# Splitting weights on VectorE instead of GpSimd in the later stages of an attention, feed-forward and expert kernel, with three weight blocks split early

## The chip, the cores and the metric

The kernel runs on one core of one Trainium2 chip. The metric is device time in microseconds (us) of one execution, lower is better. The core has TensorE (PE in the rows, with PEld for its weight loads), VectorE (DVE), ScalarE (ACT), GpSimd (POOL) and SyncE (SP, which issues most transfers). Each engine works through its own instructions in the order of the program and waits for the others by semaphores.

## The reference

Three parts follow one another; the output of each is the input of the next.

```python
# 1. attention: batch 4, 8 heads, 1152 keys, head size 64; queries pooled in twos
q_pool = q.reshape(B, H, S // 2, 2, D).mean(axis=3)
scores = scale * q_pool @ k^T;  attn = softmax(scores);  x = attn @ v      # x: 2304 tokens x 512
# 2. feed-forward on all tokens, 512 -> 2048 -> 512, w_in and w_out are float64
h = x @ w_in;  g = h * sigmoid(1.702 * h);  x = g @ w_out
# 3. experts: tokens with x @ w_skip > 0 go to the best of 8 experts, the rest stay as they are
out = x;  out[sel] += gate * (relu(x[sel] @ w1[e]) @ w2[e])                 # 512 -> 1024 -> 512
```

## The kernel before, in words

Products are made from two parts of each operand, a high one (the operand rounded to the 4-byte type that TensorE multiplies) and a low one (the rest), so that `a*b` is taken as `ah*bh + ah*bl + al*bh`. Making the two parts is called a split: ScalarE writes the high part, and VectorE or GpSimd writes the low one. `nc.gpsimd` is GpSimd, `V` is VectorE.

**Attention** (`attention`, L124) goes over 16 pairs of heads. One pair has 14 score units (`UNITS`, `NU`), and a counter `g` runs over all units. At each `g` the loop at L365 issues one score unit (matmuls, then an exponential on ScalarE into tiles `E`), one unit of row maxima for a pair 19 units ahead (matmul, then a VectorE reduction, L230), now and then the product with `v` (L306), and a unit of row sums: GpSimd adds up the tiles `E` (`sum_unit`, L284 and L286) and finishes the denominators `ds` (through the agenda, so that their line is L69). `den` (L316) turns `ds` into the matmul `dn`. Other work hangs on the agenda `ag`, a list of (step, function) run when `g` reaches the step; `quiet` picks steps with little VectorE work.

**Splitting float64 weights** (`wsplit`, L422). The weights come as pairs of 32-bit words. A unit `u` is one of 32 tiles of 128 x 512 weights (w_in or w_out of one of 16 blocks `fb`). It takes seven VectorE operations on words (L450, L451, L452, L440, L454, L455, L444), two ScalarE copies (L441 for the low words, L446 for the high part) and one product for the low part (L445), which GpSimd makes for all blocks but block 0. With `EARLY = 1` the two units of block 0 are split during attention (`weights`, L341); the other thirty are split in the first chunk of the feed-forward stage, whose buffers (`m_raw`, `m_tmp`) are opened after attention is closed.

**Feed-forward** (`ffn`, L484). The 2304 tokens go in six chunks (`CH`: 768, 384, 256, 256, 256, 384). The first has 32 steps (16 blocks, two pieces of 384 tokens); a step is `layer1` (12 matmuls into `h`, then sigmoid on ScalarE, `g = h * g` on VectorE, the high part `gh` on ScalarE, the low part `gl`: GpSimd in the first chunk, VectorE later) and, two steps behind, `layer2` (9 matmuls). There are two `h` buffers, so that the matmuls of a step need the `g` of the step two before. `fill(k)` issues the next k waiting VectorE items between these. In the first chunk one unit of weights is split in each step, and the high part of a unit is put into the next step (`ag.at(ag.now + 1, put)`). The tokens of the next chunk are loaded, normalised (`xnorm`, on GpSimd) and split in the last blocks.

**Experts** (`experts`, L841). Slots follow one another, one expert each, with tiles of up to 128 tokens (`tokens_tile`, L908): 24 matmuls up, relu, transposes, 24 matmuls down, `yo` (L957), and a scatter by GpSimd. In the first tile of a slot the 16 weight tiles of the next expert are split (`splits`, L892; L800 is the high part on ScalarE, L801 the low one); every third low part is GpSimd's, which also issues the gathers (L867) and scatters (L958) of tokens. A VectorE operation writes the second half of the relu (L947).

## Time and profile before

| | us |
|---|---|
| median of 3 runs (lowest to highest) | 1119.11 (1115.97 to 1127.57) |
| the profiled execution's own time | 1114.21 |
| its span, from the first to the last instruction | 1112.4 |
| attention, 0 to 450.5: PE / DVE / POOL busy | 433.71 / 324.39 / 383.67 |
| first chunk of feed-forward, 450.5 to 625.3 | 145.33 / 157.21 / 80.39 |
| other chunks, 625.3 to 903 | 275.66 / 199.75 / 31.26 |
| experts, 903 to 1112.4 | 163.18 / 125.56 / 85.74 |

The rows further down are of four kinds. A row of a timeline is: start, duration (us), engine, line, operation, output and inputs with their shapes, a count, and in brackets how long the engine sat idle before it and what ended that. A row of a stretch is: the stretch, its length, then for PE, PEld, DVE, ACT and POOL the busy time with the number of instructions, the granted TensorE clock (1.00 is full speed), the DMA share and GB/s. A row of waits is: engine and line, what it waited for, total us, times, longest. A row of a line is: engine, operation, count, then minimum, median and maximum duration in ns, first and last start, shape.

### The profile page before, as it was taken

The page shows a single profiled execution, that of the slowest core. Times are in us where ns is not written, and L with a number is a line of the kernel's source. Part 1 is how long each engine was busy: PE and PEld are TensorE (multiplying, and loading weights), DVE is VectorE, ACT ScalarE, POOL GpSimd, SP SyncE. Part 2 cuts the span into 40 slices and gives each one's busy share as a digit, 9 for nine tenths or more (in the row PEclk, how much of TensorE's full clock was granted, in tenths as well). Part 3 has the DMA queues.
Part 4 walks back from the last instruction along what each step waited for, and adds up shares of the span by engine and source line. Part 5 has one row for each costly group of instructions (what it writes and reads, how often), then busy time and mean ns, then how long its engine had stood idle before and what let it go on. Part 6 is the DMA issues. An engine that isn't in the chain of part 4 may idle for free. (4 is left out here: it accounts for less than half of the span.)

```text
span 1112.4 us, 19158 instructions
## 1 busy us (share of the span) xinstructions
PE 1017.9 (91%) x7002; PEld 801.3 (72%) x7002; DVE 806.9 (73%) x1584; ACT 482.1 (43%) x885; POOL 581.1 (52%) x408
## 2 busy tenths in 40 slices
PE   6999999999999999688978999999999989977893
PEld 4766767666776666587867898888889877755672
DVE  6767787778877772699999589787567555578734
ACT  2555555555555545243333332333332334256432
POOL 3698888998999988444445202101110106156413
PEclk9999999999999999889999999999999989988897
DMA  4233332223333210332333420211211326456301
GB/s 154 66 95 80 92 108 77 76 90 91 92 108 93 71 48 27 125 96 95 105 117 100 143 77 20 69 62 31 66 41 55 111 92 215 149 184 214 112 31 39
DMA packets 64325, 103.39 MB, mean 93 GB/s; under 512 B 18630, under 2 KB 34630, under 8 KB 64072
## 3 DMA queue, kind: packets, MB, share of 16 engines
q1 hardware_dynamic: 60148, 96.35, 27.4%
q0 software_dynamic: 3904, 5.15, 1.5%
q8 instruction: 69, 1.13, 0.4%
q14 instruction: 56, 0.46, 0.1%
q10 hardware_dynamic: 148, 0.30, 0.1%
HBM read 90.04 MB, written 17.35 MB: 97 GB/s over the span
## 5 line engine op out<-in xcount | busy, mean ns | idle before, releaser
L230 DVE TENSOR_REDUCE mx<-xs 128x1 f32<-128x384 f32 x432 | 213.0, 549 | 79.5 <-PE xs L227 74.8
L271 ACT ACTIVATE E<-ss 128x640 f32<-128x640 f32 (+1 forms) x224 | 174.0, 786 | 155.3 <-PE ss L270 123.0
L286 POOL TENSOR_TENSOR acc<-acc,E 128x640 f32<-128x640 f32 (+1 forms) x96 | 182.1, 1897 | 19.5 <-ACT E L271 15.4
L563 PE MATMUL h<-xh,wih 128*128 128x384 f32 (+1 forms) x448 | 145.8, 326 | 30.8 <-ACT wih L446 26.0
L306 PE MATMUL av<-E,v 128*64 128x256 f32 (+1 forms) x1152 | 157.1, 413 | 0.0
L563 PE MATMUL h<-xl,wih 128*128 128x384 f32 (+1 forms) x448 | 143.6, 321 | 0.7 <-DVE xl L482 0.6
L563 PE MATMUL h<-xh,wil 128*128 128x384 f32 (+1 forms) x448 | 143.2, 320 | 0.0
L563 PEld LDWEIGHTS h<-xh,wih 128*128 128x128 f32 x448 | 86.7, 194 | 43.0 <-ACT wih L446 31.7
L306 PEld LDWEIGHTS av<-E,v 128*64 128x64 f32 x1152 | 75.7, 136 | 56.0 <-issue 15.1
L587 PE MATMUL acc<-woh,gh 128*128 128x512 f32 x288 | 115.6, 401 | 0.0
L589 PE MATMUL acc<-woh,gl 128*128 128x512 f32 x288 | 115.2, 400 | 0.0
L588 PE MATMUL acc<-wol,gh 128*128 128x512 f32 x288 | 114.9, 399 | 0.0
L227 PE MATMUL xs<-kh,qh 64*128 64x384 f32 x384 | 102.3, 389 | 9.7 <-ACT kh L207 7.2
L270 PE MATMUL ss<-qh,kh 64*128 64x320 f32 (+1 forms) x576 | 107.1, 340 | 0.9 <-ACT E L271 0.9
L270 PE MATMUL ss<-M,ONE 64*128 64x320 f32 (+1 forms) x576 | 95.0, 296 | 2.5 <-DMA M<-ml 2.3
L569 DVE TENSOR_TENSOR g<-h,g 128x384 f32<-128x384 f32 (+1 forms) x112 | 55.8, 498 | 56.0 <-ACT g L568 51.3
L606 DVE CUSTOM_DVE_ANT_0 junk<-xs,wg 128x512 bf16<-128x512 f32 x135 | 94.7, 701 | 2.0
L658 POOL DMA_INDIRECT LIST<-pay,si x18 | 18.3, 1018 | 143.0 <-DVE si L655 75.6
L270 PE MATMUL ss<-qh,kl 64*128 64x320 f32 (+1 forms) x576 | 92.4, 294 | 0.0
L270 PE MATMUL ss<-ql,kh 64*128 64x320 f32 (+1 forms) x576 | 92.4, 294 | 0.0
L568 ACT ACTIVATE g<-h 128x384 f32<-128x384 f32 (+1 forms) x112 | 49.1, 439 | 99.1 <-PE h L563 98.8
L563 PEld LDWEIGHTS h<-xl,wih 128*128 128x128 f32 x448 | 87.0, 194 | 5.2 <-DVE xl L482 1.2
(196 smaller groups left out, 2176.8 us busy)
## 6 DMA issues: line engine op xcount, KB each, us to landing
stage<-w SPq DMA_DIRECT2D x40, 512.0 KB
qd<-qT SPq DMA_DIRECT2D x16, 576.0 KB
v<-v SPq DMA_DIRECT2D x16, 576.0 KB
kr<-kT SPq DMA_DIRECT2D x15, 576.0 KB
wr<-w_in SPq DMA_DIRECT2D x15, 512.0 KB
wr<-w_out SPq DMA_DIRECT2D x15, 512.0 KB
X<-xs SPq DMA_DIRECT2D x18, 256.0 KB
out<-xs SPq DMA_DIRECT2D x18, 256.0 KB
```

Source lines behind the costliest of these rows:

```text
L227: nc.tensor.matmul(ps[:, :384], q, k[:, part * 384:part * 384 + 384], start=True, stop=True)
L230: V.reduce_max(o, ps[:, :384], axis=AX.X)
L270: nc.tensor.matmul(ps[:, u, j * w:j * w + w], k[HALF[u]], q[HALF[u], qs], start=(n == 0), stop=(n == 3))
L271: nc.scalar.activation(place(p, i), ps[:, :, :len(kbs) * w], AF.Exp, scale=0.5 / D ** 0.5)
L286: G.tensor_tensor(d["a"], d["a"], place(p, i), op=ALU.add)
L306: nc.tensor.matmul(d["av"][HALF[u], :w], d["v"][:, u, kb], e[:, u, n * w:n * w + w], start=(kb == 0), stop=(kb == KB - 1))
L563: nc.tensor.matmul(h, a[:, d * P:d * P + P], x, start=(k == 0), stop=(k == 3 * ND - 1))
L569: V.tensor_tensor(g, h, g, op=ALU.mult)
L587: nc.tensor.matmul(acc[t], gh[:, ts], bh, start=(fb == 0), stop=False)
L588: nc.tensor.matmul(acc[t], gh[:, ts], bl, start=False, stop=False)
L589: nc.tensor.matmul(acc[t], gl[:, ts], bh, start=False, stop=(fb == NF - 1))
L606: V.tensor_tensor_reduce(out=junk, in0=R[grp[i]], in1=late["wg"][:, e], op0=ALU.mult, op1=ALU.add, scale=1.0, scalar=0.0, accum_out=R[grp] ...
```

## The change

It has six parts.

1. **Buffers.** The buffers for weight words as loaded (`raw`, three of them) are opened before attention and live until the first chunk ends, so that loads can be issued during attention.
2. **Three early blocks.** `EARLY` is 3. The two units of block 0 are split where they were; units 2 to 5 are loaded and split beside the last pair of heads, from 5 units before it to its end. The loads of units 6 and 7 are issued there too.
3. **A unit's operations.** The first word operation (the absolute value) goes from VectorE to ScalarE (`AF.Abs`), the product for the low part from GpSimd to VectorE. VectorE still has seven operations for a unit. In the first chunk they come from a generator, `blocks`, that takes two units in turn and is not bound to a step: 6 or 7 items in each step.
4. **Feed-forward without GpSimd in the first chunk.** `gl` is always VectorE's, and so is `xnorm` for the second chunk; its load and its split are moved by a step or two.
5. **The end of attention.** For the last pair the sums of units 10 to 13 and the denominators are VectorE's (`G = V`).
6. **Experts.** All 16 low parts of a slot are VectorE's; the second half of the relu is ScalarE's.

```diff
-EARLY = 1
+EARLY = 3
@@ sum_unit
+            G = V if p == N - 1 and i > 8 else nc.gpsimd
@@ attention, agenda
-        for b in range(2 * EARLY):
-            ag.at(NU * 1 + 3 + b * (NU * 3 + 6), weights, b // 2, b % 2)
+        for u in range(2):
+            g = NU * 1 + 3 + u * (NU * 3 + 6)
+            ag.at(g, self.wload, u)
+            ag.at(g + 6, weights, u, lambda j, f: quiet(AV_AT[3:], j, f))
+
+        for u in range(2, 2 * EARLY):
+            g, n = NU * (N - 1) - 5, u - 2
+            ag.at(g - 13 + 4 * n if n < 3 else g + 7, self.wload, u)
+            ag.at(g + 5 * n, weights, u, lambda j, f, g=g + 5 * n: ag.at(g + j * 5 // 7, f))
+        for n in range(2):
+            ag.at(NU * N - 8 + 5 * n, self.wload, 2 * EARLY + n)
@@ wsplit
         def last():
-            V.tensor_scalar(sg, t2, 0xFF800000, None, op0=ALU.bitwise_and)
-            (nc.gpsimd if fb else V).tensor_tensor(lo_t, t1.bitcast(F32), sg.bitcast(F32), op=ALU.mult)
-            put = lambda: nc.scalar.activation(hi_t, t2.bitcast(F32), AF.Copy)
-            put() if ag is None else ag.at(ag.now + 1, put)
+            nc.scalar.activation(hi_t, t2.bitcast(F32), AF.Copy)
+            V.tensor_tensor(lo_t, t1.bitcast(F32), sg.bitcast(F32), op=ALU.mult)
-            lambda: V.tensor_scalar(t2, hi, 0x7FFFFFFF, None, op0=ALU.bitwise_and),
+        nc.scalar.activation(t2.bitcast(F32), hi.bitcast(F32), AF.Abs)
@@ ffn
+        def blocks():
+            end = ()
+            for u in range(2 * EARLY, 2 * NF):
+                if u + 2 < 2 * NF:
+                    self.wload(u + 2)
+                a, b, c, d, e, *new = self.wsplit(u, [tp.tile([P, 512], U32, name=nm, tag=nm) for nm in ("t1", "t2", "sg")])
+                yield from (a, *end[:1], b, c, d, *end[1:], e)
+                end = new
+            yield from end
-            self.xnorm(xa[c, j, pc], xraw.pop((c, j, pc)), c, j, pc, nc.gpsimd)
+            self.xnorm(xa[c, j, pc], xraw.pop((c, j, pc)), c, j, pc, V if c == 1 else nc.gpsimd)
-            (nc.gpsimd if c == 0 else V).tensor_tensor(gl, g, gh, op=ALU.subtract)
+            V.tensor_tensor(gl, g, gh, op=ALU.subtract)
-                    wsplit(2 * (fb + EARLY) + 1 + pc)
-                    fa, fb_ = 3, 4
+                    fa, fb_ = 3, 3 + pc
-                            g0 = first[0, 10] + 2 * j if c == 0 else first[c, 4] + 2 * j
+                            g0 = first[0, 12] + 2 * j - 1 if c == 0 else first[c, 4] + 2 * j
@@ experts
-                lambda q=q: self.expert_split(s, q, stage[q // 2][:, q % 2], nc.gpsimd if q % 3 == 2 else V)
+            return [lambda q=q: self.expert_split(s, q, stage[q // 2][:, q % 2]) for q in range(16)]
-            V.tensor_scalar(h[:, 512:], hp[1], 0.0, None, op0=ALU.max)
+            nc.scalar.activation(h[:, 512:], hp[1], AF.Relu)
```

In the first chunk of the feed-forward stage VectorE had, in the second step, the seven word operations of one unit in a row (`t` and `sg` are scratch tiles, `wr` the words as loaded), and then the `g` of the next step:

```order
L569 TENSOR_TENSOR g<-h,g 128x384
L450 TENSOR_SCALAR t_6185<-wr 128x512
L451 TENSOR_SCALAR t_6184<-wr 128x512
L452 TENSOR_SCALAR t_6185<-t_6185 128x512
L440 SCALAR_TENSOR_TENSOR t_6184<-wr,t_6184 128x512
L454 TENSOR_SCALAR t_6185<-t_6185 128x512
L455 SCALAR_TENSOR_TENSOR t_6185<-wr,t_6185 128x512
L444 TENSOR_SCALAR sg<-t_6185 128x512
L569 TENSOR_TENSOR g<-h,g 128x384
```

Now it has there, after `g` (L583), parts of two units, the product `wil` among them, and `gl`:

```order
L583 TENSOR_TENSOR g<-h,g 128x384
L455 TENSOR_SCALAR sg<-t_6241 128x512
L464 TENSOR_SCALAR t_6254<-t_6254 128x512
L451 SCALAR_TENSOR_TENSOR t_6253<-wr,t_6253 128x512
L586 TENSOR_TENSOR gl<-g,gh 128x384
L466 TENSOR_SCALAR t_6254<-t_6254 128x512
L459 TENSOR_TENSOR wil_6150<-t_6240,sg 128x512
L467 SCALAR_TENSOR_TENSOR t_6254<-wr,t_6254 128x512
L463 TENSOR_SCALAR t_6288<-wr 128x512
L583 TENSOR_TENSOR g<-h,g 128x384
```

What moved: one operation on `wr` and its own result has left VectorE, `gl` and the product have come, and no operation reads the result of the one just ahead of it.

At the start of the last pair of attention ScalarE had only exponentials, a split of tokens (`xh`), and the copy `ev`:

```order
L271 ACTIVATE E<-ss 128x640
L478 ACTIVATE xh_85<-xraw 128x384
L271 ACTIVATE E<-ss 128x640
L310 ACTIVATE ev<-av 128x256
L271 ACTIVATE E<-ss 128x640 x7
```

Now the ScalarE operations of a unit of weights stand between the exponentials (L461 absolute value, L452 low words, L458 high part):

```order
L274 ACTIVATE E<-ss 128x640
L461 ACTIVATE t<-wr 128x512
L491 ACTIVATE xh_93<-xraw 128x384
L274 ACTIVATE E<-ss 128x640
L314 ACTIVATE ev<-av 128x256
L452 ACTIVATE t<-t 128x512
L274 ACTIVATE E<-ss 128x640 x3
L458 ACTIVATE woh_79<-t 128x512
L274 ACTIVATE E<-ss 128x640
```

What moved: L452 and L458 wait for VectorE, and the exponentials behind them wait with them.

In the first tile of an expert slot VectorE had eleven low parts (L801; five more were GpSimd's); from the first `hT` on:

```order
L929 TENSOR_TENSOR hT_10709<-pq0_10734,hT_10709 128x512
L801 TENSOR_TENSOR wil11_6051<-stage3_10715,wih11_6050 128x512
L947 TENSOR_SCALAR h_10708<-hp1_10733 128x512
L906 TENSOR_TENSOR xT2_10707<-pt1_10731,xT2_10707 128x512
L801 TENSOR_TENSOR wol11_6053<-stage3_10715,woh11_6052 128x512
L929 TENSOR_TENSOR hT_10709<-pq1_10735,hT_10709 128x512
```

Now it has all sixteen (L809), and no relu:

```order
L934 TENSOR_TENSOR hT_10701<-pq0_10726,hT_10701 128x512
L809 TENSOR_TENSOR wol10_6124<-stage2_10706,woh10_6123 128x512
L809 TENSOR_TENSOR wil11_6118<-stage3_10707,wih11_6117 128x512
L911 TENSOR_TENSOR xT2_10699<-pt1_10723,xT2_10699 128x512
L809 TENSOR_TENSOR wol11_6120<-stage3_10707,woh11_6119 128x512
L809 TENSOR_TENSOR wil12_6114<-stage4_10708,wih12_6113 128x512
L934 TENSOR_TENSOR hT_10701<-pq1_10727,hT_10701 128x512
```

What moved: between the two `hT` stand four low parts where there were two, and the relu is gone; ahead of the first `hT` there are five where there were four, and behind the second seven where there were five.

## Rows read from the trace of the kernel before

**Rows 1.** One stretch, the first chunk of feed-forward.

```profile
450.50:625.30 174.80, 145.33 (x656) 127.15 (x654) 157.21 (x245) 64.91 (x127) 80.39 (x72) 0.93 0.35 113
```

**Rows 2.** Waits of PE between 460 and 620 us.

```profile
PE h L563 <- ACT wih L446: 26.0, 13, 4.4
```

**Rows 3.** Timeline of DVE over one step of that chunk.

```profile
474.33 0.56 DVE L569 TENSOR_TENSOR g<-h,g 128x384 f32<-128x384 f32 x1
474.80 1.12 DVE L450 TENSOR_SCALAR t<-wr 128x512 uint32<-128x512 uint32 x1
475.85 1.22 DVE L451 TENSOR_SCALAR t<-wr 128x512 uint32<-128x512 uint32 x1
...
479.67 0.56 DVE L569 TENSOR_TENSOR g<-h,g 128x384 f32<-128x384 f32 x1
```

**Rows 4.** Timeline of POOL over the same step.

```profile
474.34 1.30 POOL L445 TENSOR_TENSOR wol<-t,sg 128x512 fp32r<-128x512 f32 x1 [2.89 <-ACT g L568]
475.60 1.19 POOL L572 TENSOR_TENSOR gl<-g,gh 128x384 fp32r<-128x384 f32 x1
```

**Rows 5.** Waits of PE in the experts, 965 to 1100 us.

```profile
PE y L937 <- DVE hT L929: 16.1, 3, 6.0
PE pq L926 <- DVE h L947: 5.3, 2, 3.6
```

**Rows 6.** Timeline of DVE in the expert slots.

```profile
971.26 0.75 DVE L957 SCALAR_TENSOR_TENSOR yo<-y,ids,xg 128x512 f32<-128x512 f32 x1 [2.83 <-PE y L937]
...
981.16 7.21 DVE L801 TENSOR_TENSOR wol<-stage,woh 128x512 fp32r<-128x512 f32 x1
...
1055.49 0.74 DVE L957 SCALAR_TENSOR_TENSOR yo<-y,ids,xg 128x512 f32<-128x512 f32 x1
```

**Rows 7.** Timeline of POOL in the first of these slots.

```profile
980.62 1.00 POOL L867 DMA_INDIRECT xg<-X,ids  x1 [0.30 <-issue]
981.63 1.31 POOL L801 TENSOR_TENSOR wil<-stage,wih 128x512 fp32r<-128x512 f32 x1
...
986.57 1.25 POOL L801 TENSOR_TENSOR wil<-stage,wih 128x512 fp32r<-128x512 f32 x1
```

**Rows 8.** Timeline of DVE in the first unit after attention, POOL idle.

```profile
455.58 0.42 DVE L452 TENSOR_SCALAR t<-t 128x512 f32<-128x512 f32 x1
455.92 0.68 DVE L440 SCALAR_TENSOR_TENSOR t<-wr,t 128x512 uint32<-128x512 uint32 x1
456.52 0.42 DVE L454 TENSOR_SCALAR t<-t 128x512 uint32<-128x512 uint32 x1
```

**Rows 9.** One line of DVE, POOL idle: low parts of the first expert.

```profile
L801 DVE TENSOR_TENSOR wil<-first,wih x8: 682/689/694, 882.9 to 896.7; 128x512 fp32r<-128x512 f32 x8
```

**Rows 10.** Timeline of PE: a `layer2`, a `layer1`, the next `layer2`.

```profile
497.58 0.40 PE L587 MATMUL acc<-woh,gh 128*128 128x512 f32 x1
...
499.69 0.34 PE L563 MATMUL h<-xh,wih 128*128 128x384 f32 x1
...
501.76 0.40 PE L587 MATMUL acc<-woh,gh 128*128 128x512 f32 x1
```

**Rows 11.** Timeline of DVE: an `xnorm` in attention that waited for its load.

```profile
432.17 1.28 DVE L469 TENSOR_TENSOR xraw<-xraw 128x384 f32<-128x384 f32 x1 [4.13 <-DMA xraw<-RD]
```

**Rows 12.** One stretch: from the last row maxima to the end of attention.

```profile
410.60:450.50 39.90, 35.35 (x353) 23.39 (x350) 9.49 (x11) 20.34 (x29) 36.00 (x28) 0.98 0.08 26
```

**Rows 13.** Lines of DVE in the early units of attention, POOL busy.

```profile
L450 DVE TENSOR_SCALAR t<-raw x2: 661/667/673, 77.0 to 182.6; 128x512 uint32<-128x512 uint32 x2
L455 DVE SCALAR_TENSOR_TENSOR t<-raw,t x2: 1535/1539/1543, 134.8 to 239.6; 128x512 uint32<-128x512 uint32 x2
L445 DVE TENSOR_TENSOR wil<-t x1: 2739/2739/2739, 156.7 to 156.7; 128x512 fp32r<-128x512 f32 x1
```

**Rows 14.** Timeline at the end of attention, POOL and PE.

```profile
442.72 2.57 POOL L286 TENSOR_TENSOR acc<-acc,E 128x1024 f32<-128x1024 f32 x1
449.39 1.23 PE L322 MATMUL dn<-ds,one 128*64 128x288 f32 x4 [1.85 <-POOL ds L69]
```

More of the change, by code (lines that the diff above doesn't have):

```diff
@@ L106, in run @@
                 self.xhl = [[xk.tile([P, 384], F32R, name=f"x{n}{i}") for i in range(8)] for n in "hl"]
+                self.rctx = mid.enter_context(ExitStack())
+                self.rp = self.pool(self.rctx, "raw", 3, side="right", reuse_waits="tile")
+                self.raws = {}
                 with ExitStack() as ctx:
@@ L339, in attention, with weights @@
                  10: [(k_high, 1, 2)], 11: [(v_load, 0)], 13: [(q_add, 2)]}
-        def weights(fb, k):
-            raw = ld.tile([P, 512], self.w_in.dtype, name="raw", tag="raw", bufs=1)
-            self.wload(raw, fb, k)
-            def split():
-                t = ld.tile([P, 3, 512], U32, name="t", tag="wt", bufs=1)
-                fq = []
-                self.wsplit(fq, raw, [t[:, 0], t[:, 1], t[:, 2]], fb, k, ag)
-                for j, f in enumerate(fq):
-                    quiet(AV_AT[3:], j, f)
-            ag.at(ag.now + 6, split)
+        def weights(u, put):
+            t = ld.tile([P, 3, 512], U32, name="t", tag="wt", bufs=1)
+            for j, f in enumerate(self.wsplit(u, [t[:, 0], t[:, 1], t[:, 2]])):
+                put(j, f)
         def operands(j, pc):
@@ L414, in wtiles, with wload @@
             self.W[fb, n] = pool.tile([P, 512], F32R, name=f"{n}{fb}")
-    def wload(self, raw, fb, k):
+    def wload(self, u):
+        fb, k = divmod(u, 2)
+        raw = self.raws[u] = self.rp.tile([P, 512], self.w_in.dtype, name="wr", tag="wr")
         if k == 0:
@@ L420, in wload, with wsplit @@
             self.dma(raw, self.w_out[fb * P:fb * P + P])
-    def wsplit(self, fq, a, tmp, fb, k, ag=None):
+    def wsplit(self, u, tmp):
         nc, V = self.nc, self.nc.vector
+        fb, k = divmod(u, 2)
+        a = self.raws.pop(u)
         hi_t, lo_t = self.W[fb, ("wih", "woh")[k]], self.W[fb, ("wil", "wol")[k]]
+        none = lambda: None
         if a.dtype == F32:
-            def plain():
-                nc.scalar.activation(hi_t, a, AF.Copy)
-                V.tensor_tensor(lo_t, a, hi_t, op=ALU.subtract)
-            fq.append(plain)
-            return
+            return [
+                none, none, none, none, none,
+                lambda: nc.scalar.activation(hi_t, a, AF.Copy),
+                lambda: V.tensor_tensor(lo_t, a, hi_t, op=ALU.subtract),
+            ]
         w = a.bitcast(U32).rearrange("p (n two) -> p n two", two=2)
@@ L520, in ffn @@
         ag = Agenda()
-        def fill(k):
-            while k and fq:
-                fq.pop(0)()
-                k -= 1
-        raws = {}
-        def wload(u):
-            if u < 2 * NF:
-                raws[u] = rp.tile([P, 512], self.w_in.dtype, name="wr", tag="wr")
-                self.wload(raws[u], *divmod(u, 2))
-        def wsplit(u, later=True):
-            if u < 2 * NF:
-                t = [tp.tile([P, 512], U32, name=nm, tag=nm) for nm in ("t1", "t2", "sg")]
-                self.wsplit(fq, raws.pop(u), t, *divmod(u, 2), ag if later else None)
+        def blocks():
[7 more added lines that the diff above has]
+            yield from end
+        splits = blocks()
+        def fill(k):
+            for _ in range(k):
+                f = fq.pop(0) if fq else next(splits, None)
+                if f:
+                    f()
         xraw, xa = {}, {}
@@ L714, in rstep @@
                 fq.append(fin)
-        for u in range(2 * EARLY, 2 * EARLY + 3):
-            wload(u)
         constants()
-        wsplit(2 * EARLY, False)
         steps = [(c, fb, pc) for c in range(len(CH)) for fb in range(NF) for pc in range(len(pieces(CH[c])))]
@@ L739, in ffn @@
                         for q in range(len(pieces(CH[c + 1]))):
-                            g0 = first[0, 10] + 2 * j if c == 0 else first[c, 4] + 2 * j
+                            g0 = first[0, 12] + 2 * j - 1 if c == 0 else first[c, 4] + 2 * j
                             ag.at(g0, xload, c + 1, j, q)
                             ag.at(g0 + 1, xnorm, c + 1, j, q)
-                            ag.at(first[c, NF - 1] + 1 if c == 0 else g0 + 4, xsplit, c + 1, j, q)
+                            ag.at(first[c, NF - 1] if c == 0 else g0 + 4, xsplit, c + 1, j, q)
             if g >= LAG:
@@ L811, in first_expert_split @@
         for c in range(2):
-            self.expert_split(0, 2 * m + c, self.first[:, m % 4 * 2 + c], self.nc.vector)
+            self.expert_split(0, 2 * m + c, self.first[:, m % 4 * 2 + c])
         if m < 4:
@@ L892, in splits @@
         def splits(s):
-            return [
-                lambda q=q: self.expert_split(s, q, stage[q // 2][:, q % 2], nc.gpsimd if q % 3 == 2 else V)
-                for q in range(16)
-            ]
+            return [lambda q=q: self.expert_split(s, q, stage[q // 2][:, q % 2]) for q in range(16)]
         def xpose(t):
```

20 lines of the change are left out of this document (10 added, 10 removed).

## The prediction, made before the changed kernel was timed

> **What bounds the kernel now.** I read the table of stretches by stage first, then, in the stages that the change touches, the waits of PE, then the timelines of the two engines that trade work.
>
> In the first chunk of feed-forward PE is busy for 145.33 of 174.80 us and DVE for 157.21 [rows 1]. The reader should see that this is a DVE bound: a step, from one `g` to the next, takes 5.34 us [rows 3], and 32 steps of 5.34 are 171 us, nearly the stage. PE's part of a step is 4.18 us, 2.11 for `layer2` and 2.07 for `layer1` [rows 10], so 32 steps could run in 133.8. PE loses 26.0 us on the high parts of `w_in` alone [rows 2], which wait for DVE's word operations and are then put off by a step. POOL makes DVE slower: L450 and L451 take 1.12 and 1.22 us [rows 3] exactly while POOL makes `wol` and `gl` [rows 4], and operations of the same kind take 0.42 with POOL idle [rows 8].
>
> In the experts, five slots split weights for the next expert. Four of them, from `yo` to `yo`, take 84.2 us, 21.1 each [rows 6]. In the first, a low part on DVE lasts 7.21 us, from 981.16 to 988.37, instead of 0.69 [rows 6, 9], and POOL's split operations run back to back beside it, from 981.63 until 987.82 [rows 7]. What stands behind the stuck operation, `hT` or the relu half, comes late: PE waits 16.1 + 5.3 = 21.4 us for them, five times, once per slot [rows 5].
>
> In attention PE is the bound, also to the end: 35.35 of the last 39.90 us, with DVE at 9.49 and POOL at 36.00 [rows 12]. Its last step waits 1.85 us for POOL's `ds` [rows 14].
>
> **First chunk without POOL.** A unit is now four one-input and two two-input operations on words, and the product. With POOL idle one starts 0.34 us after the one before (455.58 to 455.92), a two-input one takes 0.60 until the next (455.92 to 456.52): the durations overlap by 0.08 [rows 8]. The product is shaped like the low part of an expert, 0.69 less 0.08 = 0.61 [rows 9]. So 4 x 0.34 + 2 x 0.60 + 0.61 = 3.17 us, and the 26 units left are 82.4 us. `g` takes 0.47 until the next start (474.33 to 474.80 [rows 3]); `gl` has the same shape, so 32 steps are 30 us more. Four `xnorm` products add about 2. That is 115 us of DVE work in a stage whose PE work is 133.8: **PE becomes the bound**. The cover is thin, 0.6 us in a step: if the two bits of POOL work had kept DVE at its 1.12 and 1.22, it would be gone.
>
> What comes on top of 133.8 no row shows directly. Below it is nothing: units 6 and 7 are loaded, and three blocks split, before the stage begins, and the high part is no longer put off by a step, so that each reason for [rows 2] is gone. Above, all 26.0 us could come back in another form: ScalarE's low-word copy waits for DVE, and the sigmoid queued behind it then holds up `g`; and an `xnorm`, now on DVE, can wait for its load, as one in attention did for 4.13 us [rows 11], with `g` queued behind it; four of those are 16.5. I take 9, a third of the upper end, since a DVE with slack in each step catches up. The stage: 142.8 against 174.8, **-32.0** (-41.0 to -15.0).
>
> **End of attention.** Here DVE takes four units' operations while POOL is still adding up `E`. With POOL busy, a one-input operation takes 0.67, a two-input one 1.54 and the product 2.74 [rows 13]: a unit is 4 x 0.67 + 2 x 1.54 + 2.74 = 8.5 us against 3.17. I take 2.5 units at the first price and 1.5 at the second, since the sums of units 10 to 13 leave POOL: 26.0 us. These sums are some 4,800 columns on DVE, at 0.61 per 512 [rows 9] 5.8 us. With DVE's present 9.49 from 410.6 on [rows 12] it ends at 410.6 + 9.5 + 26.0 + 5.8 = 451.9, where POOL ended at 449.39 [rows 14]: **+2.5**. If all four units pay the high price, +10.5; if none does, PE's own work decides, and the 4.5 us in which it is idle there [rows 12] are the most that can be gained. ScalarE's L452 and L458 wait for DVE, with exponentials queued behind them, for which PE waits: this is how a slow DVE reaches PE before the end.
>
> One rule of the Trainium skill ("SBUF — State Buffer", section "Who interferes with whom") speaks against this part. It says that DVE and GpSimd share one pair of ports as an exclusive lock: the one that issues first has it for the whole instruction and the other fully blocks, and a DVE instruction with two SBUF inputs contends with a GpSimd instruction that reads SBUF. Taken so, each of the twelve two-input operations of the four units could wait out a whole POOL sum, 2.57 us [rows 14]; as an estimate from that, the end of attention would come at +20 instead of +2.5. The early units' 1.54 [rows 13] is 0.86 longer than 0.68 with POOL idle [rows 8], a part of a POOL sum and not the whole of it, so this trace agrees with a contention but not with that size.
>
> **Experts.** With no split on POOL, DVE's low part should last its 0.69, and the 21.4 us of PE waits [rows 5] end. DVE gets five more low parts in a slot, 5 x 0.61 = 3.1 us, and loses the relu half. Sixteen low parts are 9.8 us in a slot that would be 21.1 - 4.3 = 16.8 long, so they fit; ahead of the first `hT` stand five, one more than before, or 0.6 us later than an undisturbed `hT` would be, which the words and transposes ahead of it on PE cover. I take **-21.4**. The poor end: the gathers stay on POOL, 1.00 us each [rows 7]; if two in each slot still hold up DVE for their length, 10 us stay, -11. The good end: the stuck operation's whole excess, 7.21 - 0.69 = 6.5 in each of five slots, -33.
>
> **Sum.** The span is 1112.4. With +2.5 - 32.0 - 21.4 it is 1061.5, and with the 1.8 us by which the profiled execution's time (1114.21) exceeds its span, 1063.3. The lowest of the three runs shown is 1.8 above the profiled one, the median 4.9; I add 2: **1065 us**. All other stages keep their instructions, apart from an `xnorm` shifted by a step.
>
> **The rivals.**
> (a) *The chain through DVE and ScalarE keeps the first chunk near 160 us.* Two units in turn put more operations between `g` and `gl`, 6 or 7 in each step, and two `h` buffers leave no room: all 26.0 us of [rows 2] come back as waits for `g`. Against it: DVE has 115 us of work in the stage. 1065 + 17 = 1082.
> (b) *The last pair suffers*: +10.5 by all units at the high price, 1073; +20 by POOL's whole sums, 1083. For it: POOL is busy for 36.00 of 39.90 us there [rows 12].
> (c) *The expert slots do not shrink.* That is so if what holds the low part is its own order and not POOL's splits: gathers and scatters are still POOL's, and one ends at 981.62, just before the splits begin [rows 7]. The 21.4 us stay: 1086. The rule of the Trainium skill named above would fit this if it held by first issue: DVE's operation started at 981.16, 0.47 us before POOL's first split, so DVE should have kept the ports; it ended only after POOL's last one, so the trace disagrees with the rule here.
> (d) *PE is the bound without a gap in all three places*: the first chunk at 133.8, attention -4.5, experts past the waits of [rows 5]: 1065 - 9 - 7 - 6 = 1043.
> (e) *The other side, not faster.* In attention's last pair the twelve two-input operations starve behind POOL's sums, queued back to back, as the low parts do behind its splits in the experts: not 0.86 but 7.21 - 0.69 = 6.5 us each [rows 6, 9]. DVE would then need 9.5 + 5.8 + 12.7 + 78 = 106 us from 410.6 instead of 38.8, the exponentials behind L452 and L458 wait with it, and the end of attention moves by 67: 1065 + 64.5 = 1130. The gain elsewhere, 53.4, is eaten up at (38.8 + 53.4 - 28.0) / 12 = 5.3 us of wait for each operation. For it: POOL's queue is dense there. Against: in the early units, with POOL as busy, they took 1.54 and 2.74 [rows 13].
>
> **How the numbers follow.** The forecast 0.63, (a) 0.13, (b) 0.08, (c) 0.06, (d) 0.04, (e) 0.06. The three terms' bounds, taken as independent, give sqrt(17^2 + 8^2 + 10.4^2) = 21.5 up and sqrt(9^2 + 7^2 + 11.6^2) = 16 down, 1049 to 1087; with (c) above and (d) below the range is 1043 to 1090, which leaves out (e) and the sum of two or three of the poor cases. A measurement of this kernel can tell about 1%, 11 us, from no change. All cases but (e) are faster by more than that: 0.94. Case (e) is at the border at its own price: half of it slower by over 1%, 0.03, half, with smaller waits, within 1%, 0.03.
>
> **What would show it.** In the changed profile: in the first chunk POOL nearly idle, DVE's one-input word operations at 0.42, a `layer2` plus a `layer1` every 4.2 to 4.5 us, the stage near 143, and waits of PE for `wih` gone; waits for `g` or of DVE for a load instead would be (a). From 410.6 on, DVE's product at 2.7 or less and the first `layer1` near 453; a product of 6 us or more would be (e). In the experts, no low part on DVE over about 1.7 us, `yo` to `yo` at some 17 us, and no waits for `hT`; a slot still at 21 would be (c). The forecast is wrong as a whole if attention ends over 10 us later, or if the first chunk stays above 160.

## The result and the profile after

The changed kernel takes 1068.85 us (median of 4 runs, 1066.4 to 1071.45), the kernel before beside it 1120.48; the ratio is 0.9534, with a 95% interval of 0.9476 to 0.9592. The profiled execution took 1067.2 us, its span is 1065.1. The forecast was 1065.

The stages of the two profiled executions, each from one instruction to another (first `layer1` matmul, first `layer1` of the second chunk, first and last `yo`):

| stage, us | before | after | difference | forecast |
|---|---|---|---|---|
| attention, to the first `layer1` | 450.55 | 455.89 | +5.3 | +2.5 |
| first chunk | 174.75 | 140.99 | -33.8 | -32.0 |
| other chunks, routing, to the first `yo` | 301.5 | 302.7 | +1.2 | 0 |
| expert slots, to the last `yo` | 171.8 | 151.1 | -20.7 | -21.4 |
| to the end | 13.8 | 14.4 | +0.6 | 0 |

This is the first chunk of the changed kernel, with the columns of [rows 1].

```profile
455.89:596.88 140.99, 135.55 (x656) 119.67 (x655) 116.73 (x252) 76.68 (x144) 0.00 (x0) 0.98 0.34 106
```

It answers [rows 1]: POOL is idle, DVE is at 116.73 us instead of 157.21, and PE is busy for 135.55 of 140.99. PE is the bound now. Its waits in that chunk (456 to 601 us; engine and line, what it waited for, total, times, longest) answer [rows 2]; the 26.0 us for `wih` are gone. The single wait for `xh` lies behind the chunk's end, at 600.22.

```profile
PE h L577 <- DVE g L583: 5.3, 8, 1.8
PE h L577 <- ACT xh L491: 1.6, 1, 1.6
```

A step of DVE there, to be held against [rows 3] (start, duration, engine, line, operation):

```profile
501.28 0.56 DVE L583 TENSOR_TENSOR g<-h,g 128x384 f32<-128x384 f32 x1 [1.08 <-ACT g L582]
...
503.76 0.42 DVE L463 TENSOR_SCALAR t<-wr 128x512 uint32<-128x512 uint32 x1
...
506.52 0.56 DVE L583 TENSOR_TENSOR g<-h,g 128x384 f32<-128x384 f32 x1 [1.08 <-ACT g L582]
...
510.01 0.55 DVE L583 TENSOR_TENSOR g<-h,g 128x384 f32<-128x384 f32 x1
```

Of the two operations on `wr` that took 1.12 and 1.22, one has gone to ScalarE and the other (L463) takes 0.42, and DVE has time to wait 1.08 us for the next `g`. This step of 5.24 us is one of the longest; the next takes 3.49, and 140.99 / 32 = 4.4 us is the mean.

The end of attention is the place that got worse. Waits of PE from 395 us on, then a timeline of four engines:

```profile
PE ss L273 <- ACT E L274: 7.7, 5, 2.8
```

```profile
413.45 2.38 POOL L288 TENSOR_TENSOR acc<-E 128x1024 f32<-128x1024 f32 x1
413.74 2.64 DVE L451 SCALAR_TENSOR_TENSOR t<-wr,t 128x512 uint32<-128x512 uint32 x1
416.42 0.63 ACT L452 ACTIVATE t<-t 128x512 f32<-128x512 uint32 x1 [2.74 <-DVE t L451]
418.01 0.39 PE L273 MATMUL ss<-qh,kh 64*128 64x256 f32 x2 [2.73 <-ACT E L274]
```

This is one chain to follow: POOL's sum begins at 413.45; DVE's operation on words, begun 0.29 us later, ends 0.55 us after that sum instead of lasting its 0.68; ScalarE's copy of the low words (L452) waits 2.74 for it, the exponentials behind the copy wait too, and PE loses 2.73 us.

In the experts the slots that split weights go from 21.1 us [rows 6] to between 15.3 and 19.5. DVE in the longest of them, from `yo` to `yo`:

```profile
974.15 0.74 DVE L962 SCALAR_TENSOR_TENSOR yo<-y,ids,x_e 128x512 f32<-128x512 f32 x1
...
988.83 0.68 DVE L934 TENSOR_TENSOR hT<-pq,hT 128x512 fp32r<-128x512 f32 x1
989.43 0.68 DVE L809 TENSOR_TENSOR wol<-stage,woh 128x512 fp32r<-128x512 f32 x1
...
993.04 0.68 DVE L809 TENSOR_TENSOR wol<-stage,woh 128x512 fp32r<-128x512 f32 x1
993.64 0.74 DVE L962 SCALAR_TENSOR_TENSOR yo<-y,ids,xg 128x512 f32<-128x512 f32 x1
```

No low part is stuck any more. Behind the second `hT` DVE works without a gap until `yo`, 4.2 us of seven low parts. In all six slots with splits `yo` now follows DVE's low parts without idle time: their end is now DVE's.

### The profile page after: what moved, and what is told of

Its sections match the earlier page's. It is cut to its first block, busy times and chain, and to the rows that moved or that the text cites. A ratio compares the mean times of both kernels' runs of the same rounds, so it can differ in the third digit from the quotient of the medians.

```text
span 1065.1 us, 19053 instructions
## 1 busy us (share of the span) xinstructions
PE 1002.7 (94%) x7002; PEld 789.9 (74%) x7002; DVE 767.6 (72%) x1643; ACT 506.0 (48%) x928; POOL 453.5 (43%) x306
## 5 line engine op out<-in xcount | busy, mean ns | idle before, releaser
L290 POOL TENSOR_TENSOR acc<-acc,E 128x640 f32<-128x640 f32 (+1 forms) x94 | 179.8, 1912 | 22.4 <-ACT E L274 18.6
L577 PE MATMUL h<-xh,wih 128*128 128x384 f32 (+1 forms) x448 | 142.7, 318 | 8.7 <-DVE g L583 6.3
L577 PE MATMUL h<-xl,wih 128*128 128x384 f32 (+1 forms) x448 | 140.7, 314 | 0.2
L577 PE MATMUL h<-xh,wil 128*128 128x384 f32 (+1 forms) x448 | 140.5, 314 | 0.0
L482 POOL TENSOR_TENSOR xa<-xraw 128x256 f32<-128x256 f32 (+1 forms) x16 | 14.2, 890 | 256.9 <-DMA xraw<-RD 251.4
L577 PEld LDWEIGHTS h<-xh,wih 128*128 128x128 f32 x448 | 84.9, 190 | 18.8 <-DVE g L583 11.1
L583 DVE TENSOR_TENSOR g<-h,g 128x384 f32<-128x384 f32 (+1 forms) x112 | 55.8, 498 | 59.4 <-ACT g L582 58.0
L584 ACT ACTIVATE gh<-g 128x384 fp32r<-128x384 f32 (+1 forms) x112 | 53.8, 480 | 89.9 <-DVE g L583 89.9
```

What stands on the lines that cost most here:

```text
L290: G.tensor_tensor(d["a"], d["a"], place(p, i), op=ALU.add)
L577: nc.tensor.matmul(h, a[:, d * P:d * P + P], x, start=(k == 0), stop=(k == 3 * ND - 1))
L583: V.tensor_tensor(g, h, g, op=ALU.mult)
```

## The experiments

All twelve, with four of the five stretches (each from the profiled execution; the median is that of 3 to 10 runs):

| kernel | median | attention | first chunk | to first `yo` | slots |
|---|---|---|---|---|---|
| before | 1119.11 | 450.6 | 174.8 | 301.5 | 171.8 |
| changed | 1068.85 | 455.9 | 141.0 | 302.7 | 151.1 |
| `pool_chunk` | 1090.95 | 456.1 | 161.9 | 305.5 | 151.3 |
| `before_chunk_v` | 1104.29 | 451.4 | 160.7 | 302.3 | 167.5 |
| `before_hi` | 1114.68 | 451.5 | 171.4 | 302.4 | 176.0 |
| `early1` | 1078.11 | 444.4 | 166.9 | 301.4 | 150.2 |
| `early2` | 1070.11 | 452.4 | 150.6 | 301.4 | 150.3 |
| `one_unit` | 1085.91 | 459.0 | 148.7 | 305.2 | 156.9 |
| `low_late` | 1069.45 | 456.5 | 138.5 | 305.6 | 151.4 |
| `sums_pool` | 1072.30 | 463.3 | 140.0 | 307.8 | 144.9 |
| `spread` | 1080.65 | 471.8 | 140.1 | 304.8 | 148.2 |
| `mixed` | 1077.06 | 461.1 | 138.4 | 309.4 | 152.8 |
| `pool_exp` | 1075.06 | 457.9 | 138.5 | 305.8 | 156.0 |
| `relu_v` | 1074.25 | 458.9 | 140.9 | 302.9 | 154.7 |

The expectations reckon the chunk to a later point: they have 144.4 us for the changed kernel where the table has 141.0, and 169 for `early1` where it has 166.9.

The table also tells how far one stretch can be read: attention with the same instructions ends between 455.9 and 459.0 (`pool_chunk`, `pool_exp`, `relu_v`, `one_unit` and the changed kernel), first chunks with the same instructions take 138.4 to 141.0, and slots with the same instructions 144.9 to 156.9. Differences inside these bounds are not read below, other than at like clocks. Much of the spread goes with the granted clock (the third number from the end of a row of a stretch). These are the slots of `sums_pool` and of `one_unit`, the two ends of the last range:

```profile
911.09:1056.01 144.92, 133.78 (x628) 105.96 (x628) 92.11 (x148) 82.24 (x153) 37.16 (x36) 0.98 0.52 171
912.93:1069.85 156.92, 139.45 (x628) 110.06 (x628) 92.15 (x148) 82.30 (x153) 38.95 (x37) 0.93 0.49 160
```

**The first chunk: GpSimd's two operations back.**

```diff
-            V.tensor_tensor(gl, g, gh, op=ALU.subtract)
+            (nc.gpsimd if c == 0 else V).tensor_tensor(gl, g, gh, op=ALU.subtract)
-            V.tensor_tensor(lo_t, t1.bitcast(F32), sg.bitcast(F32), op=ALU.mult)
+            (nc.gpsimd if fb >= EARLY else V).tensor_tensor(lo_t, ..., op=ALU.mult)
```

> The changed kernel, but in the first feed-forward chunk gl and the product for the low part are GpSimd's again (xnorm, the early blocks, the absolute value on ScalarE and the two units in turn stay). Theory (GpSimd's two operations slow VectorE's beside them): one-input word operations beside them go from 0.42 to 1.1 us or more, VectorE's busy time in the chunk stays at 117 or rises to 140 although it has 58 operations fewer, worth some 31 us; the chunk takes 150 to 165 us instead of 144.4, the kernel 1075 to 1090. Rival (the new order and the early blocks made the gain, contention is small): VectorE's busy time falls to about 90, the chunk stays at 143 to 146, the kernel at 1067 to 1071.

Its chunk, and then two lines of DVE in it (busy us, mean ns); they took 682 and 418 ns each in the changed kernel:

```profile
456.09:617.99 161.90, 141.22 (x656) 121.75 (x655) 133.16 (x195) 76.57 (x144) 74.56 (x57) 0.96 0.29 90
```

```profile
L451 DVE SCALAR_TENSOR_TENSOR t<-wr,t 128x512 uint32<-128x512 uint32 x26 | 35.2, 1356 | 0.0
L466 DVE TENSOR_SCALAR t<-t 128x512 uint32<-128x512 uint32 x26 | 18.3, 702 | 0.0
```

The kernel went to 1090.95, 1 us over the theory's range, the chunk to 161.9, and TensorE waited 20.7 us for `g` in 18 places. DVE has 57 instructions fewer and is busy for 16 us longer. The theory holds, though a mean one-input operation grew to 0.50 to 0.70, since only those that stand beside POOL's operation are slowed, one at 500.28 to 1.25 us.

The same from the other side: the kernel before, with these two operations moved to the engine that bounds it.

```diff
-            (nc.gpsimd if fb else V).tensor_tensor(lo_t, ..., op=ALU.mult)
+            V.tensor_tensor(lo_t, ..., op=ALU.mult)
-            (nc.gpsimd if c == 0 else V).tensor_tensor(gl, g, gh, op=ALU.subtract)
+            V.tensor_tensor(gl, g, gh, op=ALU.subtract)
```

> The kernel before, but in the first chunk gl and the product are VectorE's: GpSimd's two operations of a step go to the engine that was the bound. Theory (GpSimd's operations cost VectorE more time than they save it): VectorE's word operations fall to 0.42 and 0.68, a step needs 5 x 0.34 + 2 x 0.60 + 0.61 + 2 x 0.47 = 4.45 us of VectorE instead of 5.34, and the chunk takes 150 to 168 us instead of 174.8, the upper end if the missing lead counts as in the run with EARLY = 1 (167); the kernel takes 1092 to 1113. Rival (an engine that is the bound gets slower by what it is given): 32 x (0.61 + 0.47) = 35 us more, 1145 to 1155.

```profile
451.42:612.15 160.73, 141.12 (x656) 123.26 (x654) 146.45 (x306) 64.87 (x127) 5.35 (x10) 0.95 0.38 122
```

DVE has 306 instructions instead of 245 [rows 1] and is busy for 146.45 us instead of 157.21; the chunk is 14 us shorter and the kernel 1.4% faster, 1104.29 (ratio 0.9862, 0.981 to 0.9914). This edit alone is less than half of the chunk's gain. The rest is left to the lead and the order, which are tried below, to ScalarE's absolute value, which was not tried by itself, and to the loads: here, as in the kernel before, the first operation on words starts 4.4 us into the chunk, when its load has landed; in the changed kernel it is loaded during attention. TensorE still waits 16.0 us for `wih`.

```profile
455.85 0.43 DVE L450 TENSOR_SCALAR t<-wr 128x512 uint32<-128x512 uint32 x1 [11.91 <-DMA wr<-w_in]
```

**The first chunk: what the 26.0 us for `wih` were.** In the kernel before, the high part at once instead of a step later:

```diff
-            put() if ag is None else ag.at(ag.now + 1, put)
+            put()
```

> The kernel before, but the high part of a unit is written at once instead of in the next step. Theory (VectorE bounds the chunk, and TensorE's 26.0 us of waits for wih are how that shows): these waits turn into waits for g, the step stays at 5.2 to 5.4 us, the chunk takes 168 to 175 us, the kernel 1112 to 1120. Rival (the put-off is what makes TensorE wait): the 26.0 us go, the chunk takes 149 to 155, the kernel 1094 to 1100.

Its chunk, and the waits of PE in it:

```profile
451.50:622.87 171.37, 139.90 (x657) 116.31 (x655) 143.70 (x245) 68.15 (x127) 79.63 (x75) 0.99 0.35 110
```

```profile
PE h L563 <- DVE g L569: 31.4, 30, 2.6
```

No wait for `wih` is left, 31.4 us for `g` stand in its place, and the time is the same (1114.68; ratio 1.0017, 0.997 to 1.0064). So the putting-off was not what held the chunk. That DVE's own work held it is not shown by this run alone: DVE is busy for only 143.70 us here and waits 18.8 us (460 to 620 us) for ScalarE's sigmoid, which now stands behind the high part.

**The lead.** Fewer early units, with 7 items a step where there is one early block:

```diff
-EARLY = 3
+EARLY = 1        # fa, fb_ = 3, 4
```

> The changed kernel with EARLY = 1: no unit is split beside the last pair of heads; thirty units are split in the first chunk, 7 items in each step. Theory (the early units cost 5 to 7 us at the end of attention and VectorE has room for them in the chunk, 117 + 4 x 3.2 = 130 of 144 us): attention ends at 449 to 451 instead of 455.8, the chunk grows by 0 to 6 us, mostly in its first steps, where the second block must be made first; the kernel takes 1063 to 1070. Rival (the early units are what takes VectorE below TensorE): the chunk grows by the whole 12.7 us of work, to 157, the kernel takes 1074 to 1078.

Its chunk, and PE's waits in it:

```profile
444.35:611.28 166.93, 138.90 (x656) 121.23 (x655) 131.31 (x283) 89.51 (x159) 0.00 (x0) 0.96 0.33 109
```

```profile
PE h L577 <- ACT wih L458: 22.0, 14, 5.3
```

Neither case had it. Attention ends at 444.35, 11.5 us earlier, so that the four early units cost twice what I had put; but the chunk takes 166.9. DVE has no more work than forecast (131.31, and less than PE's 138.90), yet PE waits for 14 blocks' `wih`, and DVE waits for ScalarE's sigmoid ahead of `g` in turn (29.0 us): each unit is finished just when it is wanted, and the two sides wait for each other by turns. Nine more us in all.

```diff
-EARLY = 3
+EARLY = 2
```

> The changed kernel with EARLY = 2: two units instead of four beside the last pair. The run with EARLY = 1 ended attention at 444.3, 11.5 us earlier, and took 169 us for the chunk. Theory (what counts in the chunk is the lead, how many units VectorE is ahead of TensorE, and two units of lead last nearly to its end at 6.5 items a step): attention ends at 449 to 452, the chunk takes 144 to 150, the kernel 1063 to 1069. Rival (the chunk grows with the work that is left to it, (169 - 144.4) / 4 = 6.1 us for each unit): chunk 156, the kernel 1074 to 1077.

Attention 452.35, chunk 150.6, the kernel 1070.11, as near to the changed kernel as can be told. TensorE waited 13.2 us for `wih` in 8 places, 9.3 of them after 542 us: most of the chunk goes by before a lead of two units less is used up, at 6.5 items a step where a unit a step would be 7. The 3.5 us saved in attention are more than given back in the chunk, 9.6 longer, but the medians are 1.3 apart: the trade is flat, or nearly so, between two blocks and three.

**Two units in turn.** One unit after the other, in the changed kernel:

```diff
-                yield from (a, *end[:1], b, c, d, *end[1:], e)
-                end = new
+                yield from (a, b, c, d, e, *new)
```

> The changed kernel, but in the first chunk the seven operations of a unit stand in a row, one unit after the other, instead of two units in turn. Theory (VectorE, at 117 of 141 us, has room for the waits that this brings): VectorE waits 0.3 to 0.9 us in each unit for ScalarE's absolute value or low words, up to 20 us in all, of which the chunk sees 0 to 6; the kernel takes 1067 to 1075. Rival (the two units in turn are what keeps VectorE ahead of TensorE): the lead is used up, TensorE waits for wih as with EARLY = 1, the chunk takes 152 or more, the kernel 1080 or more.

The chunk takes 148.7, 7.7 us more, with 10.9 us of waits for `g` and none for `wih`: the lead isn't used up, and DVE's work is 121.46. That is a little above the theory's 6 and not the rival's. The kernel's 1085.91 is 17 above the changed one and outside the theory's range; the other 9 us lie in stretches whose instructions this edit leaves alone: attention, the other chunks and the slots, each at a lower granted clock than in the changed kernel. For attention this can be followed. Two stretches of five us of the last pair, each first in this kernel, then in the changed one:

```profile
430.00:435.00 5.00, 5.00 (x34) 2.94 (x34) 3.18 (x3) 1.71 (x4) 1.54 (x1) 0.66 0.50 136
430.00:435.00 5.00, 4.73 (x44) 3.13 (x44) 3.69 (x5) 3.33 (x7) 2.21 (x2) 1.00 0.57 156
440.00:445.00 5.00, 4.21 (x38) 3.56 (x40) 4.82 (x5) 3.66 (x6) 3.97 (x5) 0.66 0.00 0
440.00:445.00 5.00, 5.00 (x60) 3.48 (x58) 3.65 (x3) 3.49 (x6) 3.83 (x7) 1.00 0.00 0
```

At a granted clock of 0.66, a mix of 2.4 and 1.2 GHz, PE does 34 and 38 matmuls where it does 44 and 60 at 1.00. As an estimate, 0.34 of 5.00 us twice is 3.4 us; attention is 3.1 longer. In the five us before the first stretch, 425 to 430, PE was busy for 2.03 of 5 in this kernel and for 2.29 in the changed one: a gap of nearly the same size was followed by the lower clock in one and not in the other. What decides this stayed open.

**The end of attention.** ScalarE's copy of the low words one score unit later:

```diff
-            nc.scalar.activation(t1.bitcast(F32), t1, AF.Copy, scale=2.0 ** -43)
+            conv = lambda: nc.scalar.activation(t1.bitcast(F32), t1, AF.Copy, scale=2.0 ** -43)
+            later(conv) if later else conv()        # later: ag.at(ag.now + 1, f)
```

> The changed kernel, but for the four units beside the last pair of heads ScalarE's copy of the low words (L452) is issued one score unit later, so that one more exponential stands ahead of it. Theory (TensorE's 7.7 us of waits for E at the end of attention come from the exponentials queued behind L452, which waits 9.1 us for VectorE's L451): these waits fall to 3 us or less, attention ends 3 to 5 us earlier, the kernel takes 1064 to 1066. Rival (VectorE's own work decides the end, by ds): the waits for E fall, but attention ends within 1 us of 455.8, the kernel takes 1068 to 1070.

Its timeline, with rows of POOL, DVE, ScalarE and PE:

```profile
413.77 2.40 POOL L288 TENSOR_TENSOR acc<-E 128x1024 f32<-128x1024 f32 x1
414.06 2.65 DVE L451 SCALAR_TENSOR_TENSOR t<-wr,t 128x512 uint32<-128x512 uint32 x1
...
416.24 5.22 POOL L290 TENSOR_TENSOR acc<-acc,E 128x1024 f32<-128x1024 f32 x2
416.63 2.60 DVE L467 TENSOR_SCALAR t<-t 128x512 uint32<-128x512 uint32 x1
419.27 2.74 DVE L468 SCALAR_TENSOR_TENSOR t<-wr,t 128x512 uint32<-128x512 uint32 x1
...
422.04 0.63 ACT L459 ACTIVATE wih<-t 128x512 fp32r<-128x512 f32 x1 [3.27 <-DVE t L468]
...
428.72 0.64 PE L273 MATMUL ss<-qh,kh 64*128 64x320 f32 x2 [4.55 <-ACT E L274]
```

1069.45: no gain, and attention ends at 456.5. The first wait went and the next one took its place: now POOL's sums followed each other without a gap, DVE got through one operation for each of them, the one-input one too, and ScalarE stood at the high part (L459) instead, with PE's waits for `E` at 6.5 us in all. The rival's time, but not its picture: waits for `E` fell by 1 us only. By these rows, what sets this stretch is DVE's pace beside POOL.

The sums of the last pair back to GpSimd:

```diff
-            G = V if p == N - 1 and i > 8 else nc.gpsimd
+            G = nc.gpsimd
```

> The changed kernel, but the last pair's sums and denominators are GpSimd's again; the four early units stay beside it. Theory (GpSimd's dense queue holds VectorE's operations, and its slower sums end last): word operations of 1.5 to 3 us also in the fourth unit, TensorE waits 2 to 4 us for ds, attention ends 3 to 8 us after 455.8, the kernel takes 1072 to 1077. Rival (what the sums cost VectorE is what they cost GpSimd): attention ends within 1.5 us of 455.8, 1067 to 1071.

Attention ends at 463.3, 7.4 us later, TensorE waits 4.8 us for `ds` (the theory said 2 to 4), the kernel takes 1072.3: the theory, though the kernel lost less than the stretch; its slots were the shortest of all, within what the table says can't be read.

The early units elsewhere. All six over the pairs 1 to 15, three steps a pair:

```diff
-        for u in range(2):
+        for u in range(2 * EARLY):
...
-            ag.at(g + 6, weights, u, lambda j, f: quiet(AV_AT[3:], j, f))
+            ag.at(g + 6, weights, u, lambda j, f: quiet(AV_AT[1::2] + AV_AT[4:], j, f))
... (the loop over units 2 to 5 goes)
```

> The changed kernel with EARLY = 3, but all six early units are split one after the other over the pairs 1 to 15, at three steps of each pair, none packed beside the last pair. Theory (VectorE has room in the earlier pairs, where TensorE waits for almost nothing, and the lead in the chunk is what is needed): attention ends at 444 to 447, the chunk stays at 143 to 146, the kernel takes 1056 to 1062. Rival (attention has no room for them: each operation held up by GpSimd's sums delays the row maxima, and TensorE with them): the 11 us come back spread over attention, 1066 to 1072.

Four over the pairs 1 to 14 at the two steps of before, two beside the last pair:

```diff
-        for u in range(2):
+        for u in range(4):        # one after the other, 44 and 54 units apart
...
-        for u in range(2, 2 * EARLY):
+        for u in range(4, 2 * EARLY):
```

> The changed kernel with the same six early units, but four of them one after the other over the pairs 1 to 14, at the two steps of each pair that units 0 and 1 had, and only two beside the last pair. Theory (what made the spread run slow was the step ahead of the row maxima, not the early units as such; two packed units cost about half of four): attention ends at 449 to 453 as with EARLY = 2, the chunk keeps its lead and its 139 to 142 us, the kernel takes 1060 to 1066. Rival (any unit beside GpSimd's sums costs attention about 3 us, wherever it stands): attention ends at 455 to 459, the kernel takes 1068 to 1072.

Waits of PE from 100 to 460 us, first of `spread`, then of `mixed`:

```profile
PE xs L230 <- DVE mx L233: 13.2, 13, 2.2
```

```profile
PE xs L230 <- DVE mx L233: 8.3, 11, 1.3
```

In the changed kernel this wait is 0.2 us, in one place. Both kernels are slower, 1080.65 and 1077.06, and attention ends 16 and 5 us later than in the changed one; the rival was right in both, and the sizes were worse than it said. TensorE is the bound all through attention and DVE's row maxima are just in time, so each early operation that POOL's sums hold up is felt at once. Beside the last pair there are no row maxima left. The chunk is at 138 to 140 in both: the lead is the same wherever the units are made. No variant beat the changed kernel.

**Experts, a square of two edits.** Every third low part back to GpSimd, and, apart from it, the second half of the relu back to VectorE:

```diff
-            return [lambda q=q: self.expert_split(s, q, stage[q // 2][:, q % 2]) for q in range(16)]
+            return [lambda q=q: self.expert_split(s, q, ..., nc.gpsimd if q % 3 == 2 else V) for q in range(16)]
```

> The changed kernel, but in the experts every third low part is GpSimd's again, as before the change; the second half of the relu stays on ScalarE. Theory (VectorE's low part waits out GpSimd's splits, and hT behind it): low parts on VectorE of 3 to 7 us are back, TensorE waits 10 to 20 us for hT, the slots with splits grow by 2 to 4 us each, the kernel takes 1080 to 1092. Rival (the relu half that left VectorE, or the gathers, made the difference): slots as in the changed kernel, 1066 to 1071.

```diff
-            nc.scalar.activation(h[:, 512:], hp[1], AF.Relu)
+            V.tensor_scalar(h[:, 512:], hp[1], 0.0, None, op0=ALU.max)
```

> The changed kernel, but the second half of the relu in the experts is VectorE's again; all low parts stay on VectorE. With the run that put every third low part back on GpSimd (+6 us), it completes a square of two edits whose sum is 20 us. Theory (the two work together: a relu queued on VectorE is late only where a low part ahead of it is held up by GpSimd): a relu waits for at most two low parts, 1.2 us, the six slots with splits grow by 0 to 1.2 us each, the kernel takes 1069 to 1076. Rival (the relu's move by itself is the larger part of the gain): +12 to +15, 1081 to 1085.

Waits of PE in the experts, first with the low parts back, then with the relu back (before: [rows 5]; in the changed kernel there is none for `hT` on DVE):

```profile
PE y L942 <- DVE hT L934: 7.7, 5, 5.0
```

```profile
PE y L942 <- DVE hT L934: 1.4, 5, 0.3
```

The slots take 171.8 us with both edits undone, 156.0 and 154.7 with one undone, 151.1 with none. Either edit alone brings 16 or 17, the second one 4 or 5 more, which is inside what can be read. So `relu_v` came out as the theory had it (1074.25), and `pool_exp` between its two cases (1075.06; the theory said 1080 to 1092, the rival 1066 to 1071). At like clocks the two are not equal: the slots of `pool_exp` ran at 0.97, where those of `sums_pool` and `spread`, with the changed kernel's instructions, took 144.9 and 148.2 at 0.98; those of `relu_v` ran at 0.94, where those of `mixed` took 152.8. As far as this goes, the low parts are the larger piece. DVE and POOL of `pool_exp` in one slot, and then DVE in the last slot with splits, tell why it was cheaper than the theory:

```profile
972.86 0.69 DVE L934 TENSOR_TENSOR hT<-pq,hT 128x512 fp32r<-128x512 f32 x1
...
974.94 6.88 DVE L809 TENSOR_TENSOR wil<-stage,wih 128x512 fp32r<-128x512 f32 x1 [0.19 <-ACT wih L808]
...
974.02 1.00 POOL L875 DMA_INDIRECT xg<-X,ids  x1 [0.30 <-issue]
975.04 1.31 POOL L809 TENSOR_TENSOR wil<-stage,wih 128x512 fp32r<-128x512 f32 x1
...
979.98 1.28 POOL L809 TENSOR_TENSOR wil<-stage,wih 128x512 fp32r<-128x512 f32 x1
```

```profile
1046.33 6.43 DVE L809 TENSOR_TENSOR wol<-stage,woh 128x512 fp32r<-128x512 f32 x1
1052.69 0.68 DVE L934 TENSOR_TENSOR hT<-pq,hT 128x512 fp32r<-128x512 f32 x1
```

In each of the six slots with splits a low part is stuck, for 6.0 to 6.95 us, as before, beside five splits. In five of them it stands behind the second `hT` (972.86 in the first rows) and not ahead of it, so that only low parts and `yo` wait for it. In the sixth it stands ahead of `hT`; there TensorE waits the 5.0 us, and from `yo` to `yo` the slot takes 21.1 us, no less than the last one of the kernel before (20.6). So it is the place of the stuck operation in the queue, and not its length, that made it cheap.

## Why the prediction was right, and where not

**First chunk, -32.0 forecast, -33.8 measured.** The working held by its parts: DVE 115 us of work, 116.73 measured; PE 133.8, 135.55; 9 us of losses, 5.4. `pool_chunk` and `before_chunk_v` show, in both directions, that it was POOL's two operations that slowed DVE's. The granted clock rose too, from 0.93 to 0.98, but it was not what held the chunk: `before_hi` had 0.99 and took 171.37. What the working lacked is the lead. I had argued that PE becomes the bound since 115 is under 133.8. With one early block DVE's 131.31 is still under PE's 138.90, and the chunk takes 166.9. The three blocks stood in my text only as a reason why nothing comes on top; three instead of one are worth some 26 us of the chunk (166.9 - 141.0) for 11.5 us in attention. Rival (a) named a chunk near 160 and waits for `g`; that comes about with one early block, by waits for `wih`.

**End of attention, +2.5 forecast, +5.3 measured; right in kind, half of what came.** The step that failed is that DVE would work through its share without a gap. The prices held: the four units took 27.6 us of DVE (26.0 forecast), the first of them 8.5, and from 410.6 us to its end at 455.2 DVE was busy for 38.65 us (41.3 forecast). First that stretch, then the operation behind ScalarE's absolute value (L461), from 400 to 456 us (busy us, mean ns, idle time before it):

```profile
410.60:455.20 44.60, 33.84 (x325) 22.23 (x321) 38.65 (x43) 25.13 (x40) 26.55 (x25) 0.96 0.20 64
```

```profile
L464 DVE TENSOR_SCALAR t<-t 128x512 f32<-128x512 f32 x4 | 4.2, 1039 | 6.6 <-ACT t L461 6.6
```

DVE was idle for 6 us of the stretch, most of it there, and so ended at 455.2 instead of 451.9. L461 stands behind exponentials that wait for PE, and PE lost 7.7 us to exponentials that stand behind ScalarE's copies, which wait for DVE: three engines waiting in a ring. The prediction named the copies and gave the ring no time. The +5.3 is two large pieces of opposite sign: the sums on VectorE bring 6.2 us (450.55 to 444.35 in `early1`), the four units cost 11.5. With the same instructions attention ended at up to 459.0, so the miss can also be read as larger.

The rule in the Trainium skill that I had set against this part ("SBUF — State Buffer", "Who interferes with whom", the lock on the shared ports) gave the size of a single wait better than my rows of the early units: 2.60 to 2.74 us in `low_late` for an operation beside sums of 2.4 to 2.6. The page of the Trainium skill also counts the one-input `tensor_scalar` among those that can take the shared pair, and `low_late` agrees with 2.60 where 0.42 was its length alone. As an estimate for the whole, +20, it was too high, since only some of the operations met a sum: the means of the four units lie between 0.42 and 2.37 us.

**Experts, -21.4 forecast, -20.7 measured; right in kind, the closeness is luck.** The waits of [rows 5] went as forecast and low parts on DVE take 0.63 to 0.76 us. But -21.4 was the sum of these waits alone. The slots before and after:

```profile
926.80:1098.64 171.84, 142.63 (x628) 111.73 (x628) 114.90 (x128) 78.11 (x143) 76.60 (x66) 0.91 0.45 144
899.58:1050.70 151.12, 136.64 (x628) 107.69 (x628) 92.19 (x147) 82.30 (x153) 37.75 (x36) 0.95 0.50 165
```

PE's idle time fell by 14.7 us (29.2 to 14.5), since other waits grew; the other 6.0 are its busy time, for the same 628 matmuls at a granted clock of 0.95 instead of 0.91, which the sum did not have. And slots with the same instructions differ by up to 12 us. I had put the whole on POOL's splits, with the relu as a few tenths of DVE time; the square shows that moving the relu alone brings much of it too: the stuck operation, which in the kernel before stood ahead of an `hT` or the relu in five of six slots, stands behind the second `hT` in five of six. Rival (c), the slots stay as they are, fell: they shrink with either edit. Its sentence on the ports needs a qualification: in `pool_exp` DVE's operation began 0.10 us before POOL's first split and ended 0.56 after its last one, but POOL was not idle when it began, a gather ran until 975.02. The trace still disagrees with the rule of the Trainium skill in this: the five splits all began later than DVE's operation, and all went ahead of it.

**The other side**, rival (e), needed 5.3 us of wait for each two-input operation in the last pair. The longest was 2.85 less 0.69. It was at no time near.

**The rest.** The other stages moved by +1.2 and +0.6, where nothing was forecast. For the step from the profiled execution to the median I added 2 us; it was 1.65.

## What to carry to other kernels

Before work is split between VectorE and GpSimd, read what VectorE's operations cost beside GpSimd's: here the bound engine became faster by taking the work back. When one engine prepares operands for another, compare not only the sums of their work but how many items the one is ahead; a lead of two more blocks was worth more (26 us) than the work in them (131.31 - 116.73 = 14.6), and it can be bought where the other engine's critical input is already done. A stuck operation costs what stands behind it in its queue, so that moving one small operation off that queue can be worth much of what removing the cause is worth.

## What was new about the hardware

- One VectorE operation can be held through several GpSimd operations: 6.88 us through five of 1.26 to 1.31 in the experts, although all five began after it. Beside attention's sums VectorE got one operation through for each sum, 2.65, 2.60 and 2.74 us. What tells the two apart was not tried.
- One-input VectorE operations are held as well, 2.60 us instead of 0.42.
- The same instructions ran at different granted clocks from kernel to kernel: 34 matmuls in five us at 0.66 in `one_unit` where the changed kernel did 44 at 1.00, after gaps of nearly the same size (PE busy for 2.03 and 2.29 of five us), and slots of 144.92 us at 0.98 and 156.92 at 0.93.
